# Softcap attention followed by a layer of attention experts: keys transposed by DMA, two pairs of heads at a time, from the eleventh pair on

## The chip, the cores and the metric

The kernel runs on one core of one Trainium2 chip, as one program with one launch. The metric is device microseconds of an execution; lower is better. The time of a kernel is the median of several executions.

## The reference

The first part is attention with a soft cap, for 8 batches of 12 heads with 448 positions and 64 columns a head. Its output is the input x of the second part, a layer of four attention experts with causal attention; a gate picks two of the four for each position.

```python
# part 1: q, k, v are (8, 12, 448, 64) float32, cap = 30
scores = scale * q @ k.T                      # scale = 1 / sqrt(64)
scores = cap * tanh(scores / cap)
attn   = softmax(scores)
x      = (attn @ v).transpose(0, 2, 1, 3).reshape(8, 448, 768)

# part 2: four experts e, 64 columns each
logits = x @ w_gate                           # (8, 448, 4)
topk   = the two largest of the four;  w = softmax over these two
for e in range(4):
    q, k, v = x @ wq[e], x @ wk[e], x @ wv[e]
    a  = softmax(causal(scale * q @ k.T))
    ye = a @ v @ wo[e]                        # (8, 448, 768)
    out += (e in topk) * w[e] * ye
```

The output is (8, 448, 768) in float32.

## The kernel before, in words

**Pairs.** Part 1 goes by pairs of heads: 6 pairs a batch, 48 in all, numbered from 0. A pair goes through these steps. Its q, k and v are loaded by DMA on SyncE's queue (SP), two pairs with one set of DMAs, into four staging buffers (`load`). GpSimd (POOL) casts them to 16 bits: the first 384 positions of the keys (`k16`, L620), q (`q16`, L623), the 64 positions that are left of the keys of both heads as one tile of 128 columns (`ktz`, L635), and v likewise (L639, L644). `tr` then turns q and the keys on TensorE, four transposes of q (L653) and four of the keys (L663: three blocks of `k16` and one of `ktz`), into one PSUM bank, from which VectorE copies 960 columns to a buffer `qk` (L683): 448 columns of q, then 512 of keys. There are six such buffers.

**Scores and exponentials.** `fill` issues the score matmuls from `qk` (`heads` L717, `tails` L727) into two PSUM regions, X of three banks and Y of two. ScalarE reads them with tanh (L768), three instructions a pair: X with 1344 columns, Y with 896, Y again with 896. The exponential of the whole pair follows as one instruction of 3136 columns (`expo`, L780), between two of the next pair's tanh. `pv` multiplies with v on TensorE (L795, L802) and VectorE divides by the row sums (L823, L826); `xt` turns the result on TensorE (L841) and copies it (L850), which gives x with its columns on the partitions.

**Batches.** When the six pairs of a batch are done, part 2 of that batch is spread over the pairs that follow: values and gate logits (`b_v`, L910), the gate on VectorE and POOL (`b_gate`, L974 to L986), a mask that holds the gate weights, cast on POOL (L1028) and turned by a DMA transpose to `mT`; queries and keys of two experts at a time (`b_qk`, L937, the queries then multiplied with the mask, L951); the causal scores of one slot of two experts (`b_score`, L1057) into banks of region X; their exponential on ScalarE (L1066); the product with the values (`b_pv`, L1116, L1131), the sum of two experts on POOL (L1141) that a DMA transpose turns to `oT`; the output product (`b_wo`, L1164), its copies to `ob` (L377) and the stores (L1178). The helper `turned` (L389) issues both kinds of DMA transposes on SP's queue: eight blocks of 128 by 128 in one DMA for a mask, four for an output sum.

At which pair a slot's scores and exponential stand is set by a table: slots 0 and 1 of a batch come at the offsets 5 and 6 after the batch's end, for batch 6 at 6 and 7, which is pair 48 and pair 49:

```python
XOFF = (5, 6)
exps = {HP * (b + 1) + (XOFF if b < LB - 1 else (6, 7))[s]: (b, s) for b in range(LB) for s in range(2)}
```

**The last batch.** Pairs 42 to 47 have only their first 320 query columns in region X and Y; the 128 columns that are left of each go three pairs at a time through two pseudo-pairs, 48 and 49. After them `last` and `last2` do part 2 of the last batch, with a closing chain of copies and stores.

**Order.** No instruction stands where the source text has it. Each step is recorded as an operation with its engine, an assumed duration, what it reads and writes and, for some, a due time relative to one of ScalarE's tanh instructions (`ref`). ScalarE's tanh and exponentials are a fixed chain. From that chain `G.dues` derives due times for the rest, and `G.solve` then makes one list of instructions for each engine: it takes, of the operations that are ready first, the one with the smallest rank, which is the due time with a few constants and with a small shift that is drawn from `SEEDS`, one number for each 4 us. The engines run these lists in order, and semaphores hold an instruction until its inputs are there and its buffer is free. So a change in the constants, the due times or `SEEDS` moves instructions anywhere in the kernel, but each engine still does the same work.

The functions that the change touches, and what calls them:

Of the kernel before, what the change touches and what calls it, by code (L numbers as in the profile page):

```python
# [22 lines left out]
SEEDS = (0, 0, 677, 325, 935, 794, 478, 0, 0, 908, 702, 455, 94, 0, 415, 476, 0, 612, 697, 64, 320, 0, 337, 707, 93, 0, 0, 917, 365, 771, 130, 0, 644, 11, 733, 810, 0, 8, 0, 0, 56, 391, 495, 0, 0, 0, 0, 0, 0, 579, 0, 0, 472, 59, 74, 554, 0, 0, 795, 949, 933, 285, 781, 323, 0, 548, 585, 976, 176, 0, 938, 86, 0, 0, 687, 0, 992, 980)  # L23
TWIRE = 0.2
TOCC = 0.18
# [3 lines left out]
KEEPN = 1  # L29
NFILL = 30  # L30
# [19 lines left out]
class Graph:  # L50
# [79 lines left out]
    def solve(self, when, banks, lent):  # L130
# [44 lines left out]
        while len(order) < n:  # L175
            best = None
            for e, rs in ready.items():
# [8 lines left out]
                def rank(x):  # L186
# [3 lines left out]
                    d = u.due + lag if u.first or left < TAIL else max(u.due + lag, t0 + 1.223)  # L190
                    d -= 0.505 * (u.grp is not None and not u.opens and left >= TAIL)
# [5 lines left out]
                near = t0 + (0.007 if left >= TAIL else SWITCH + 0.02)  # L197
                t, o = min((x for x in c if x[0] <= near), key=rank)
                if e in ("PE", "DVE") and not o.first:
                    for t2, u in c:  # L200
                        if u.first and u.due + lag < t + o.occ + 0.0 and t2 < t + max(SWITCH + 0.01, min(o.occ, 0.25)):
                            t, o = t2, u
                            break
# [66 lines left out]
def kernel(  # L270
# [116 lines left out]
    def turned(n, dst, src, r, w, name, due=None):  # L387

        sp(lambda: nc.sync.dma_start_transpose(  # L389
            dst().rearrange("p (n t) -> p n t", t=128), src()), r, w, due, name,  # L390
           wire=TWIRE * n, occ=0.4 + TOCC * n)

# [11 lines left out]
    vtz = [sb(f"vtz{i}", [128, 2, Dh + 1]) for i in range(NV)]  # L404
    qk = [sb(f"qk{i}", [128, S + 512]) for i in range(NQK)]
# [59 lines left out]
    def load(p, n):  # L465
# [13 lines left out]
        def tail(eng, dst, src, g):  # L479
# [4 lines left out]
        sp(lambda: full(kf[s][:, d], k[b, h, 0:KM], KC), w=w("kf"), name=f"ldk{p}", wire=0.8 * n)  # L484
        sp(lambda: nc_eng.dma_start(qf[s][:, d], q[b, h].rearrange("h (p c) d -> p h (c d)", c=QC)),
           w=w("qf"), name=f"ldq{p}", wire=0.95 * n)
# [8 lines left out]
        sp(lambda: full(vf[s][:, d], v[b, h, 0:KM], KC), w=w("vf"), name=f"ldv{p}", wire=0.8 * n)  # L495
# [119 lines left out]
    def cast(p):  # L615
# [5 lines left out]

        def qc(e):
# [6 lines left out]
        else:  # L629
            gp(0.45, lambda: kc(nc.gpsimd.tensor_copy), *kio, name=f"k16_{p}")  # L630
        if p < 4:
            dve(0.48, lambda: qc(nc.vector.tensor_copy), *qio, name=f"q16_{p}", lat=0.56)
        else:
            gp(0.56, lambda: qc(nc.gpsimd.tensor_copy), *qio, name=f"q16_{p}")
        gp(0.2, lambda: nc.gpsimd.tensor_copy(ktz[z], ktf[s][:, o].rearrange("p g d -> p (g d)")),  # L635
           [("ktf", x, 0), ("ktf", x, 1), ("zk", s)], [("ktz", z)], name=f"kt16_{p}")
# [10 lines left out]
    def tr(p):  # L647
# [29 lines left out]
        g = Group(AUX)  # L677
        pe(0, lambda: tk(g, (0, 1, 2)), kr + [("s", XB[0])] * (p == 1), [("tps", p, "k"), ("qkw", t)], g, occ=0.165, name=f"trk{p}")
# [27 lines left out]

    def heads(p, what):
        dst = X if what == "X" else Y
        ci = {"X": 0, "Y1": 1, "Y2": 2}[what]
        t = qk[of(p, what)[0] % NQK]  # L710
        n = wid(p)
        for c in (ci,) if p < NP else range(KC):
            for g in range(2):
# [4 lines left out]
                    dst[:, g, o], t[r, S + 128 * (c + 1) : S + 128 * (c + 2)], t[r, qs],  # L718
# [3 lines left out]
    def tails(p):  # L722
        for i, m in enumerate(of(p)):
# [3 lines left out]
            nc.tensor.matmul(X[:, 2, o], t[:, S : S + 128], t[:, qs], start=True, stop=True)  # L727

    def fill(p, what):
        def rd(p, what=None):  # L730
            return [y for m in of(p, what) for y in (
                ("qk", m % NQK, "k"), ("qk", m % NQK, "q"), ("qkw", m % NQK))]
# [12 lines left out]
        if what == "X":  # L745
            if p == 0:
                tr_first_tails()
            pe(wid(p), lambda: tails(p), rd(p) + [
                ("qk", m % NQK, "t") for m in of(p)], [("s", bs[2])], name=f"sT_{p}",
# [6 lines left out]
    exps = {HP * (b + 1) + (XOFF if b < LB - 1 else (6, 7))[s]: (b, s) for b in range(LB) for s in range(2)}  # L756
# [145 lines left out]
    def b_v(b, ref):  # L902
        x = b % 2
        for n in range(4):
            g = Group(AUX + XB, 1.8)
            w = WIN[n]
            for j0 in (0, 2, 4):
                def mm(g=g, w=w, j0=j0):
# [8 lines left out]
                   due=(ref, 7.024 + 1.4 * n))  # L917
# [9 lines left out]
    def b_qk(b, ref):  # L927
        x = b % 2
        for r in range(2):
            for which in "kq":  # L930
                g = Group(AUX + XB, 2.4)
                w2 = (wq2 if which == "q" else wk2)[r]
                for j in range(NDC):
                    def mm(g=g, w2=w2, j=j, which=which):
# [10 lines left out]
                        due=(ref, 11.967 + 4.327 * r + 1.8 * (which == "q")))  # L945
# [293 lines left out]
    def last(ref):  # L1239
# [79 lines left out]
        for n in range(3):  # L1319
# [5 lines left out]
            def mm(g=g, n=n):  # L1325
                for e in range(E):
# [11 lines left out]
                   [(b, 3, "z")]), None, WIN1[n], (ref, 8.13))  # L1338
# [45 lines left out]
    def last2(ref):  # L1384
# [63 lines left out]
        for e in range(E):  # L1448
# [3 lines left out]
               gt2[3][:, 1, 0], W1, (ref, 9.393))  # L1452
# [15 lines left out]
    for p in range(NPV):  # L1468
# [13 lines left out]
        for what in order:  # L1482
            if what == "Y2" and p:
# [4 lines left out]
                xt(p - 1, (ACTS["Y1", p], 4.87))  # L1488
# [85 lines left out]
```

## Time and profile before

| | |
|---|---|
| runs | 315.44, 311.67, 313.27 us; median 313.27 |
| profiled execution | span 312.0 us, time 314.04 us |
| busy: TensorE | 280.9 us, 90% |
| busy: VectorE | 217.8 us, 70% |
| busy: ScalarE | 291.8 us, 94% |
| busy: GpSimd | 181.4 us, 58% |
| DMA queue q1 | 65.5% of 16 engines' span |
| HBM | 36.19 MB read, 11.01 MB written |
| granted TensorE clock, mean | 0.983 |

All profile times are from the start of the span, in microseconds, unless marked ns. The profile shows one execution, whose own time is the span and some 2 us around it; it is not the median of the runs. PE is TensorE's matmuls, PEld its weight loads, DVE VectorE, ACT ScalarE, POOL GpSimd, SP SyncE (SPq its queue). A row of an engine's groups reads: line, engine, operation, output and inputs with the shape, the number of instructions, busy time and mean nanoseconds of one, and last the idle time in front of them with what ended it. A row of the waits reads: waiting engine, what it waits to do, what released it, total wait, number, longest. A row of a window reads: the window and its length, then busy time and number of instructions of PE, PEld, DVE, ACT and POOL, the granted clock, the DMA share and the rate in GB/s; where it is asked for one line alone, only the engines that run this line have a column. A row of the timeline reads: start, duration, engine, line, operation, and in brackets the wait that went before.

### The profile page before, as it was taken

To read this page: it belongs to the slowest core of one execution; us is meant where nothing else is said; L and a number is where in the kernel's file an instruction comes from. 1 tells how busy PE (TensorE), PEld (TensorE's weight loads), DVE (VectorE), ACT (ScalarE), POOL (GpSimd) and SP (SyncE) were. 2 spreads that over 40 slices of the span, in tenths; PEclk is the share of its full clock that TensorE was granted. 3 is DMA by queue.
4 is the path that set the end of the run, shared out by engine and by line. 5 is a ranking of instruction groups with operands and counts; after the bars stand their busy time and mean duration, and the time that the engine had idled before them with its cause. 6 is when DMAs were issued, how large, how long until landed. Compare 5 with 4: busy or idle time off the path is not lost.

```text
span 312.0 us, 8950 instructions
## 1 busy us (share of the span) xinstructions
PE 280.9 (90%) x3476; PEld 190.4 (61%) x3476; DVE 217.8 (70%) x645; ACT 291.8 (94%) x246; POOL 181.4 (58%) x498
## 2 busy tenths in 40 slices
PE   7677689979898899989998999999999989999993
PEld 3354356658564766657655776568664866667761
DVE  2345556666764886869766877788776877786883
ACT  4699999998999999999999999999999999999562
POOL 7694436996787452984785576947866414701200
PEclk9979979998999999999999999999999999999999
DMA  6899999869976995789873698855014200531136
GB/s 183 182 227 221 297 272 253 220 168 268 251 189 159 313 272 159 187 179 255 217 164 78 201 310 196 129 162 154 2 41 146 97 2 19 87 120 60 36 148 207
DMA packets 87482, 53.29 MB, mean 171 GB/s; under 512 B 48144, under 2 KB 83728, under 8 KB 87440
## 3 DMA queue, kind: packets, MB, share of 16 engines
q1 hardware_dynamic: 87136, 52.49, 65.5%
q8 instruction: 27, 0.44, 0.6%
q10 hardware_dynamic: 304, 0.23, 0.2%
q14 instruction: 15, 0.12, 0.2%
HBM read 36.19 MB, written 11.01 MB: 151 GB/s over the span
## 4 chain that ended last, share of the span: by engine, by line
ACT 66%; PE 20%; DMA 4%; POOL 3%; issue 3%; DVE 2%; SPq 1%; ACTq 0%; POOLq 0%
ACT yp L768 34%; ACT yp L780 28%; ACT pB L1066 4%; PE A L1164 2%; DMA kf<-in_k_dram 2%; PE Y L717 2%; PE A L937 2%; PE A L910 2%; PE A L802 2%; DMA out_dram<-ob 2%; PE X L1057 1%; PE A L1116 1%; PE A L663 1%; PE A L795 1%; PE X L727 1%
## 5 line engine op out<-in xcount | busy, mean ns | idle before, releaser
L780 ACT ACTIVATE yp<-yp 128x3136 f16<-128x3136 f16 (+4 forms) x51 | 139.0, 2726 | 0.0
L768 ACT ACTIVATE yp<-Y 128x896 f16<-128x896 f32 (+2 forms) x100 | 94.6, 946 | 2.6 <-PE Y L717 2.6
L768 ACT ACTIVATE yp<-X 128x1344 f16<-128x1344 f32 (+2 forms) x50 | 65.1, 1302 | 2.5 <-PE X L727 1.5
L802 PE MATMUL A<-v,yp 128*128 128x65 f16 x1116 | 56.4, 194 | 0.0
L802 PEld LDWEIGHTS <-yp 128*128 128x128 f16 x1116 | 49.0, 98 | 5.7 <-issue 2.9
L795 PE MATMUL A<-vtz,yp 128*128 128x130 f16 x186 | 41.3, 222 | 7.9 <-ACT yp L780 3.7
L826 DVE TENSOR_TENSOR xk<-A,rca 128x256 f16<-128x256 f32 (+1 forms) x96 | 39.7, 415 | 2.9
L717 PE MATMUL Y<-qk 64*128 64x448 f16 (+2 forms) x216 | 36.2, 341 | 5.7 <-ACT yp L768 5.1
L639 POOL CAST v<-vf 128x384 f16<-128x384 f32 x48 | 24.6, 514 | 27.0 <-PE A L802 22.1
L620 POOL CAST k<-kf 128x384 f16<-128x384 f32 x47 | 23.7, 513 | 24.2 <-PE A L663 15.0
L683 DVE COPY qk<-A 128x960 f16<-128x960 f16 x47 | 29.5, 650 | 6.1 <-PE A L653 6.0
L377 DVE COPY ob<-A 128x384 f32<-128x384 f32 (+1 forms) x56 | 30.4, 554 | 4.7 <-PE A L1164 2.9
L823 DVE RECIPROCAL rca<-A 128x4 f32<-128x4 f32 (+1 forms) x96 | 17.1, 178 | 21.0 <-PE A L802 19.4
L795 PEld LDWEIGHTS <-yp 128*128 128x128 f16 x186 | 18.1, 97 | 19.7 <-ACT yp L780 9.3
L623 POOL CAST q<-qf 112x512 f16<-112x512 f32 x44 | 27.2, 619 | 2.3 <-DMA qf<-in_q_dram 2.1
L717 PEld LDWEIGHTS <-qk 64*128 64x128 f16 x324 | 15.0, 93 | 21.7 <-issue 15.5
L1164 PE MATMUL A<-wo,oT 128*128 128x384 f16 x112 | 26.2, 326 | 1.4 <-DVE xT L850 0.5
L1131 DVE SCALAR_TENSOR_TENSOR oB<-A,rcb,mw 128x256 f16<-128x256 f32 x54 | 25.5, 481 | 1.8
L850 DVE COPY xT<-A 128x448 f16<-128x448 f16 (+1 forms) x48 | 18.0, 376 | 9.9 <-PE A L841 9.5
L1141 POOL TENSOR_TENSOR oS<-oB,oB 128x512 f16<-128x512 f16 x14 | 16.1, 1154 | 14.5 <-DVE oB L1131 8.7
L1116 PE MATMUL A<-vB,pB 128*128 128x260 f16 x133 | 22.2, 275 | 1.6 <-DVE oB L1131 1.2
L653 PE MATMUL A<-ident,q 112*128 112x112 f16 x192 | 22.5, 219 | 0.0
(210 smaller groups left out, 569.8 us busy)
## 6 DMA issues: line engine op xcount, KB each, us to landing
qf<-in_q_dram SPq DMA_DIRECT2D x23, 448.0 KB, 6.0
kf<-in_k_dram SPq DMA_DIRECT2D x23, 384.0 KB, 5.2
vf<-in_v_dram SPq DMA_DIRECT2D x23, 384.0 KB, 4.9
out_dram<-ob SPq DMA_DIRECT2D x23, 384.0 KB, 3.8
out_dram<-ob SPq DMA_DIRECT2D x9, 192.0 KB, 2.9
ktf<-in_k_dram SPq DMA_DIRECT2D x46, 32.0 KB, 4.9
vtf<-in_v_dram SPq DMA_DIRECT2D x46, 32.0 KB, 4.3
ob<-in_moe_wv_dram SPq DMA_DIRECT2D x2, 384.0 KB, 4.1
```

The costliest lines, as they stand in the source:

```text
L377: (nc.scalar.copy if o.eng == "ACT" else nc.vector.tensor_copy)(dst(), src())
L623: e(q16[i], qf[s][:, h].rearrange("p h (c d) -> p c h d", c=QC))
L683: lambda: nc.vector.tensor_copy(qk[t], bank16(g)[:, 0 : S + 512]),
L717: nc.tensor.matmul(dst[:, g, o], t[r, S + 128 * (c + 1) : S + 128 * (c + 2)], t[r, qs], start=True, stop=True,)
L768: ACTS[what, p] = act(c_act(n * (b - a)), lambda: nc.scalar.activation(y[:, a:b, 0:n], src[:, 0 : b - a, 0:n], AF.Tanh, scale=isc / capf), ...
L780: act(c_act(n * (b - a), False), lambda a=a, b=b, n=n: nc.scalar.activation(y[:, a:b, 0:n], y[:, a:b, 0:n], AF.Exp, scale=capf), ks, ks, f ...
L795: nc.tensor.matmul(ps[:, n, :, :], y[:, 2, w : w + 128], vtz[u], start=(n == 0), stop=False, skip_group_check=True,)
L802: nc.tensor.matmul(ps[:, n, h, :], y[:, SLOT[c][h], w : w + 128], v16[u][:, h, c, :], start=False, stop=(c == 2), skip_group_check=True,)
L826: dve(c_dve(128 * m), lambda g=g, i=i, rc=rc, m=m: nc.vector.tensor_tensor(xk[p % NXK][:, 2 * i : 2 * i + m, :, :], view(g)[:, 0:m, :, 0:D ...
L1116: nc.tensor.matmul(bank(g)[:, 0 : E * (Dh + 1)], pB[pi][:, o : o + 128], vB[x][:, c, :, :], start=(t == 0), stop=(t == len(cs) - 1),)
L1131: dve(c_dve(E * Dh) + 0.06, lambda g=g, k_=k_, n=n: nc.vector.scalar_tensor_tensor(oB[s][:, n, :, :], view(g)[:, :, 0:Dh], rcb[k_][:, 0, : ...
L1164: nc.tensor.matmul(bank(g)[:, 0 : D // 2], oT[x][n // 2][:, r, n % 2, :], wo2[r][:, c0:c1], start=(r == 0), stop=(r == 1),)
```

## The change

**Keys.** From pair 10 on (`KD = 10`), keys are not turned on TensorE. At every even pair POOL casts the keys of this pair and of the next into one buffer `kz` of two pairs (`kcast`, two casts a pair, of the sizes that they had), and one DMA transpose of 8 blocks on SP's queue turns both pairs into a buffer `kd`. There are two buffers `kz` and three `kd`, and 19 such transposes. For these pairs `tr` has the four transposes of q alone, and the copy from PSUM has 448 columns; the score matmuls read the keys from `kd` and q from `qk`. Pairs 0 to 9 stay as they were.

**Batch 6.** Its first slot is exponentiated at pair 47, before at pair 48.

**Order.** `SEEDS` and the planner's constants are new, among them the assumed time of a DMA transpose on SP and on the DMA engines, and some due times: batch values, queries and keys, `xt`, the output product and two of the last batch. All orders are computed anew from these.

```diff
-SEEDS = (0, 0, 677, 325, ...
-TWIRE = 0.2
-TOCC = 0.18
+SEEDS = (0, 0, 321, 0, ...
+TWIRE = 0.065
+KD = 10
...
-                    d = u.due + lag if u.first or left < TAIL else max(u.due + lag, t0 + 1.223)
-                    d -= 0.505 * (u.grp is not None and not u.opens and left >= TAIL)
+                    d = u.due + lag if u.first or left < TAIL else max(u.due + lag, t0 + 1.213)
+                    d -= 0.269 * (u.grp is not None and not u.opens and left >= TAIL)
...
-                near = t0 + (0.007 if left >= TAIL else SWITCH + 0.02)
+                near = t0 + (0.0 if left >= TAIL else SWITCH + 0.02)
...
-                        if u.first and u.due + lag < t + o.occ + 0.0 and ...
+                        if u.first and u.due + lag < t + o.occ + 0.141 and ...
...
-           wire=TWIRE * n, occ=0.4 + TOCC * n)
+           wire=TWIRE * n, occ=1.25)
...
+    kz = [sb(f"kz{i}", [128, 2, 512]) for i in range(2)]
+    kd = [sb(f"kd{i}", [128, 2, 512]) for i in range(3)]
...
+        def kcast(p):
+            s, o, x, j = p // 2 % NST, p % 2, p % (2 * NST), p // 2
+            dst = kz[j % 2][:, o]
+            gp(0.45, lambda: nc.gpsimd.tensor_copy(
+                dst[:, 128:].rearrange("p (c h d) -> p c h d", h=2, d=Dh),
+                kf[s][:, 2 * o : 2 * o + 2].rearrange("p h (c d) -> p c h d", c=KC)),
+                [("kf", x)], [("kz", j % 2, o, "k")], name=f"k16_{p}")
+            gp(0.2, lambda: nc.gpsimd.tensor_copy(
+                dst[:, 0:128], ktf[s][:, o].rearrange("p g d -> p (g d)")), ...
...
-        else:
+        elif p < KD:
             gp(0.45, lambda: kc(nc.gpsimd.tensor_copy), *kio, name=f"k16_{p}")
+        elif p % 2 == 0:
+            kcast(p)
+            kcast(p + 1)
+            j = p // 2
+            turned(8, lambda: kd[j % 3].rearrange("p o c -> p (o c)"),
+                   lambda: kz[j % 2].rearrange("p o c -> p (o c)"),
+                   [("kz", j % 2, o_, y) for o_ in range(2) for y in "kt"], [("kd", j % 3)],
+                   f"kT{p}")
...
+        if p >= KD:
+            pe(0, lambda: tq(g, 0, 2), ...
+            pe(0, lambda: tq(g, 2, 4), ...
+            dve(c_dve(S, True), lambda: nc.vector.tensor_copy(qk[t][:, 0:S], bank16(g)[:, 0:S]), ...
+            return
...
+    def keysT(p):
+        return qk[p % NQK][:, S:] if p < KD else kd[p // 2 % 3][:, p % 2]
...
-                    dst[:, g, o], t[r, S + 128 * (c + 1) : S + 128 * (c + 2)], t[r, qs],
+                    dst[:, g, o], kT[r, 128 * (c + 1) : 128 * (c + 2)], t[r, qs],
...
-    exps = {HP * (b + 1) + (XOFF if b < LB - 1 else (6, 7))[s]: (b, s) for b in range(LB) for s in range(2)}
+    exps = {HP * (b + 1) + (XOFF if b < LB - 1 else (5, 7))[s]: (b, s) for b in range(LB) for s in range(2)}
...
-                   due=(ref, 7.024 + 1.4 * n))                              # b_v
+                   due=(ref, 5.158 + 1.4 * n))
-                        due=(ref, 11.967 + 4.327 * r + 1.8 * (which == "q")))   # b_qk
+                        due=(ref, 11.882 + 5.017 * r + 1.8 * (which == "q")))
-                xt(p - 1, (ACTS["Y1", p], 4.87))
+                xt(p - 1, (ACTS["Y1", p], 4.366))
-                        b_wo(bb, ACTS["Y1", p], *((12.261, 1.8) if bb < LB - 1 else (10.346, 0.5)))
+                        b_wo(bb, ACTS["Y1", p], *((13.886, 1.8) if bb < LB - 1 else (20.0, 0.5)))
```

37 lines of the change are left out of this document (24 added, 13 removed).

## The prediction

> **What bounds the kernel now.** I read the page's busy times first, then ScalarE's waits, then its timeline, then the windows of the end.
>
> ```profile
> span 312.0 us, 8950 instructions
> ...
> PE 280.9 (90%) x3476; PEld 190.4 (61%) x3476; DVE 217.8 (70%) x645; ACT 291.8 (94%) x246; POOL 181.4 (58%) x498
> ```
> ```profile
> ACT yp L768 <- PE Y L717: 2.6, 2, 1.7
> ...
> ACT yp L768 <- PE X L717: 0.9, 1, 0.9
> ...
> ACT pB L1066 <- PE X L1057: 0.7, 1, 0.7
> ```
> ```profile
> 11.59 0.92 ACT L768 ACTIVATE yp<-Y 128x896 f16<-128x896 f32 x1 [1.69 <-PE Y L717]
> ```
> ```profile
> 58.39 2.87 ACT L780 ACTIVATE yp<-yp 128x3136 f16<-128x3136 f16 x1
> ...
> 63.86 2.89 ACT L780 ACTIVATE yp<-yp 128x3136 f16<-128x3136 f16 x1
> ...
> 75.00 1.29 ACT L768 ACTIVATE yp<-X 128x1344 f16<-128x1344 f32 x1 [0.95 <-PE X L717]
> ```
> ```profile
> 273.02 2.18 ACT L780 ACTIVATE yp<-yp 128x2240 f16<-128x2240 f16 x1
> ...
> 277.26 2.21 ACT L780 ACTIVATE yp<-yp 128x2240 f16<-128x2240 f16 x1
> 280.13 1.02 ACT L1066 ACTIVATE pB<-X 128x1024 f16<-128x1024 f32 x1 [0.66 <-PE X L1057]
> ...
> 289.16 0.88 ACT L780 ACTIVATE yp<-yp 128x768 f16<-128x768 f16 x1
> ```
> ```profile
> 276.00:288.00 12.00, 11.45 (x200) 9.17 (x196) 9.20 (x32) 11.34 (x11) 1.53 (x4) 1.00 0.33 117
> 288.00:300.00 12.00, 12.00 (x139) 8.63 (x137) 9.76 (x41) 7.62 (x19) 2.26 (x2) 1.00 0.10 23
> 300.00:312.00 12.00, 7.17 (x80) 4.17 (x77) 7.00 (x22) 4.93 (x11) 0.00 (x0) 0.98 0.66 231
> ```
> The page is of one execution. Three stages are to be seen. Until 11.59 us ScalarE waits for its first scores, and the change starts at pair 10, so this stage stays. From 11.59 to 290.04 (289.16 + 0.88) ScalarE runs tanh and exponential without pause, 5.47 us a pair (63.86 less 58.39). Its idle time there is 0.95 at 75.00, 0.66 at 280.13, and hardly anything else: about 1.7 us in 278. Then 22 us of end work follow, in which PE is full (12.00 of 12) from 288 to 300 and a chain of copies and stores after 300. So work taken from PE and VectorE in the middle pays only where it ends one of these waits, or empties PE after 276.
>
> **The change part by part.** First, what leaves PE and VectorE: from pair 10 on, 38 pairs no longer pass four key transposes through PE, and their PSUM copy shrinks from 960 to 448 columns.
>
> ```profile
> L663 PE MATMUL A<-ident,k 128*128 128x128 f16 x144 | 16.3, 224 | 4.0 <-POOL k L620 2.1 <-DVE ob L377 0.7 <-DVE oB L1131 0.4
> L663 PE MATMUL A<-ident,ktz 128*128 128x128 f16 x47 | 10.7, 227 | 0.0
> ```
> ```profile
> L683 DVE COPY qk<-A 128x960 f16<-128x960 f16 x47 | 29.5, 650 | 6.1 <-PE A L653 6.0
> L674 DVE COPY qk<-A 128x448 f16<-128x448 f16 x1 | 0.4, 392 | 0.7 <-PE A L653 0.7
> ```
> PE was busy 27.0 us with 191 of these; 152 of them go, by the same mean 21.5 us at most (busy times of neighbours overlap, so less). VectorE saves 38 times 650 less 392 ns, 9.8 us. Both lie beside the unbroken ScalarE stretch, so I count nothing for them in the middle. If that cover were gone, 0.26 us a pair would be VectorE's share of the gain.
>
> Second, what is added: 19 transposes of 8 blocks on SP's queue. The casts on POOL stay as many and as large; only their place in POOL's order changes. The masks' transposes have the same shape and give the price.
>
> ```profile
> L389 SPq DMA_TRANSPOSE mT<-mB x14: 1232/1258/2520, 60.1 to 269.4; - x14
> ...
> DMA to landing us min/median/max: 2.3/2.8/5.7
> ```
> ```profile
> q1 hardware_dynamic: 2656, 0.66, 49.5%
> ```
> ```profile
> q1 hardware_dynamic: 87136, 52.49, 65.5%
> ```
> SP needs 19 times 1.26, 24 us more, spread over 200. The second fence is the DMA view from 266 to 274 us, where two and a half such transposes took 49.5% of 8 us, 3.96 us, so 1.6 us each; 19 are 30 us, a tenth of the span on top of 65.5%. What hides it is lead. There are three key buffers of two pairs each, so a transpose may start once the scores of the fifth pair before it are done and is due four pairs later, 22 us, of which landing takes 2.8 to 5.7. While that lead holds, ScalarE pays nothing. In the new order q's casts, PE's q transposes and the loads stand roughly where they stood.
> [...]
>
> Third, batch 6's first exponential moves from pair 48 to pair 47. The 0.66 wait at 280.13 goes. In its place ScalarE will ask for the scores when the exponential before it ends, at 275.20 (273.02 + 2.18).
>
> ```profile
> 264.32 1.15 POOL L1141 TENSOR_TENSOR oS<-oB,oB 128x512 f16<-128x512 f16 x1
> ...
> 266.88 2.29 POOL L1028 CAST mB<-ms 128x512 f16<-128x512 f32 x4
> ```
> ```profile
> 274.72 1.16 DVE L951 TENSOR_TENSOR qm<-A,mT 128x448 f16<-128x448 f32 x2 [0.79 <-PE A L937]
> ```
> ```profile
> 276.00:282.00 6.00, 1.39 (x18) 1.05 (x18) 1.00 0.63 220
> ```
> The last fence is the score matmuls of L1057 alone. Today the last masked query is ready at 275.88 and the scores take 1.39, so 277.27: unimproved, ScalarE would wait 2.07. The new order puts the 1.15 us addition behind the masks instead of into the gate, issues ten of the last twelve query matmuls before the second tanh's scores of pair 47 and gives batch 6's values an earlier due time (5.158 after 7.024). With 1.15 saved the wait is 0.92; with the PE order too it may be none. I take 0.3, bounds 0 and 2.07. Everything behind that instruction on ScalarE, two tanh of pairs 47 and 48 first, and so PE's next fills, would move with it.
> Those 1.39 us of PE also leave the window 276 to 282, just before PE is full. Of them 0.66 is the wait already counted; of the other 0.73 I take 0.4, since about as many output matmuls of batch 5 now come later (their offset goes from 12.261 to 13.886). Bounds 0 and 0.73. Further in, the gate's small exponential now stands before the last tanh on ScalarE and may wait some tenths; left in the range.
>
> Fourth, the new order elsewhere. The 0.95 at 75.00 hangs on the order of that stretch; half of it, 0.5, is taken as gain, bounds 0 and 0.95. Against it stands the clock.
>
> ```profile
> 31.64:35.06 3.42, 2.03 (x35) 1.29 (x34) 2.05 (x7) 3.42 (x3) 0.96 (x2) 1.00 1.14 323
> ...
> 38.47:41.88 3.41, 1.97 (x31) 1.44 (x32) 1.15 (x5) 3.41 (x5) 1.51 (x4) 1.00 0.94 279
> 41.88:45.30 3.42, 3.26 (x21) 1.95 (x21) 2.36 (x7) 3.42 (x4) 1.13 (x3) 0.50 1.06 302
> ...
> 65.78:69.19 3.41, 1.81 (x28) 1.25 (x25) 2.83 (x10) 3.41 (x4) 3.09 (x11) 1.00 0.66 182
> 69.19:72.60 3.41, 3.41 (x40) 2.87 (x38) 1.72 (x5) 3.41 (x3) 1.11 (x5) 0.50 0.91 240
> ...
> 137.46:140.87 3.41, 2.53 (x23) 1.44 (x23) 2.29 (x6) 3.41 (x5) 2.38 (x8) 1.00 0.77 173
> ```
> ```profile
> 137.46:140.87 3.41, 0.48 (x4) 0.34 (x4) 1.00 0.77 173
> ```
> These are steps of 3.41 us. One with PE busy 1.97 or 1.81 is followed by one at half clock, one with 2.03 is not. The half-clock step at 69.19 stands right before the 0.95 wait; the one at 41.88 cost ScalarE nothing. So a further half-clock step costs 0 to 0.95. The step at 137.46 would fall from 2.53 to 2.05 without its key transposes (second fence), almost to the edge. I count 0.3, a third of one such wait.
> [...]
>
> The sum: -0.66 + 0.3 - 0.4 - 0.5 + 0.3 = -0.96. The profiled execution has span 312.0 and time 314.04, 2.0 around the span; it becomes 311.0 and 313.1. That execution lies 0.8 above the median 313.27, so the median goes to **312.3**.
>
> **The rivals.** One, slower: keys late through SP's queue. In the new order key transposes stand directly behind mask and output transposes, and loads behind them.
>
> ```profile
> SPq L389 <- POOL oS L1141: 41.4, 5, 14.0
> SPq L389 <- POOL mB L1028: 24.1, 7, 4.7
> ```
> SP already stands up to 14.0 us at such a wait. The lead less landing is 16 to 19 us; where 14.0 and one more wait of 4.7 come together, 18.7, the keys miss their pair by up to 2.5 us and ScalarE stands that long. Two such places give 5.0, and with -0.96 a time of 317.3. For it speaks that a held transpose holds the loads too; against it, that 14.0 arose at the end with nothing queued behind. It decides from a hold of 16 us.
>
> Two, slower: the clock. Four more half-clock steps at 0.95 instead of 0.3 in the sum give +3.5 and 315.8; two give 313.9. For: the step at 137.46. Against: the lightest steps after 72 us hold few key transposes, and two of three drops cost nothing.
>
> Three, faster: all waits after 11.59 end and PE's relief counts in full: 0.66 + 0.95 + 0.73 and the further 0.2 of small gaps, 2.5, giving 310.7; with 0.6 more in the closing chain, 310.1.
>
> Four, the change does not do what it says: batch 6's first scores are not ready a pair sooner. ScalarE waits 2.07 instead of 0.66, +1.4 and no gain in the tail, 314.7 with nothing else gained.
>
> **How the numbers follow.** Chances: forecast 0.48, keys late 0.16, clock 0.10, all waits gone 0.18, not ready 0.08. ScalarE's unbroken stretch holds the gain to about 1%; only a loss can be large. About 1%, 3.1 us, is what a measurement of this kernel tells from no change (its three runs go from 311.67 to 315.44). Faster by more than that: all of the third rival's better half and a little of the forecast, 0.19. Slower: keys late and half of the clock case, 0.22. Within: 0.59. The range goes from 309.6 (the third rival less half a microsecond of spread) to 316.8 (most of the first).
>
> **What would show it.** Right: ScalarE still spaced 5.47 a pair; no wait on a key transpose among ScalarE's and PE's waits; batch 6's first exponential right behind the exponential of pair 46, its wait under 1 us; the PSUM copies near 392 ns; 47 transposes of some 1.26 us on SP with landing near 2.8. Wrong: ScalarE waiting for scores whose PE instruction waits for DMA; more half-clock steps than three before the end; PE's full stretch after 288 longer than 12 us. If ScalarE's last exponential ends later than 290, the forecast of a gain is wrong whatever the end does.

## The result, and the profile after

The changed kernel is slower: 326.69 us (median of 4 runs, 325.7 to 327.89) against 312.47 us in the same runs (311.39 to 315.44), a ratio of 1.0441 [1.0357, 1.0525]. The forecast was 312.3. Medians here and below are of all executions, while ratios leave out the few in the chip's slower state, so that a ratio need not be the quotient of two medians.

From the page: its span, the busy times, the granted clock by slices and the row of the DMA queue:

```profile
span 324.6 us, 8665 instructions
...
PE 278.3 (86%) x3324; PEld 181.8 (56%) x3324; DVE 207.8 (64%) x643; ACT 293.7 (90%) x248; POOL 181.7 (56%) x498
...
PEclk9999999989799799999959999999999999999999
...
q1 hardware_dynamic: 107200, 57.47, 72.7%
```

PE and DVE do less, and the busy share of every engine is lower than before: the kernel waits more. The queue's packets took 72.7% of 324.6, 236.0 us, where they took 65.5% of 312.0, 204.4 us.

ScalarE's waits, with the last exponentials of its main stretch:

```profile
ACT yp L803 <- PE Y L751: 14.2, 13, 3.4
...
ACT yp L803 <- PE X L751: 2.2, 3, 1.7
```
```profile
298.65 1.05 ACT L1101 ACTIVATE pB<-X0X1s 128x1024 f16<-128x1024 f32 x1
...
300.35 2.58 ACT L815 ACTIVATE yp<-yp 128x1920 f16<-128x1920 f16 x2
```

ScalarE now ends its stretch at 302.93, before at 290.04: 12.9 us later. The rest of the span is 21.7 us, before 22.0. So the whole loss lies ahead of the last exponential, and nearly all of it is waits for scores: 14.2 and 2.2 us, where before they came to 2.6 and 0.9. Without those of the first 12 us they are 14 waits with 14.5 us, where the kernel before has 0.95 and 0.66.

Where they stand, in the windows of 60 us (PE, PEld, DVE, ACT, POOL busy, clock, DMA share, GB/s), first of the kernel before, then of the changed one:

```profile
60.00:120.00 60.00, 53.90 (x684) 37.78 (x682) 41.77 (x120) 59.05 (x45) 43.02 (x111) 0.97 0.87 229
120.00:180.00 60.00, 56.89 (x712) 38.40 (x710) 46.47 (x129) 59.79 (x45) 38.67 (x98) 1.00 0.72 180
180.00:240.00 60.00, 57.30 (x705) 39.15 (x702) 45.76 (x135) 59.99 (x47) 42.97 (x108) 1.00 0.57 142
```
```profile
60.00:120.00 60.00, 50.02 (x585) 33.25 (x583) 35.84 (x109) 53.97 (x41) 36.84 (x96) 0.91 0.99 230
120.00:180.00 60.00, 48.70 (x546) 30.69 (x543) 35.87 (x110) 51.66 (x39) 37.33 (x94) 0.94 0.91 218
180.00:240.00 60.00, 55.07 (x698) 37.65 (x697) 45.30 (x138) 59.87 (x46) 37.66 (x93) 1.00 0.62 155
```

ScalarE loses 6.0 us of 60 and then 8.3, and nothing from 180 on. These are the two windows in which the DMA share is highest (0.99 and 0.91) and the clock falls. A high share alone does not make ScalarE wait, as `e15_free_keys` shows further down.

Two waits, followed back. First through the casts, in the changed kernel's timelines of POOL, PE and ScalarE:

```profile
119.37 0.51 POOL L627 CAST kz<-kf 128x384 f16<-128x384 f32 x1 [3.71 <-DMA kd<-kz]
...
123.12 0.52 POOL L1111 TENSOR_SCALAR_AFFINE_SELECT pB<-pB 128x384 f16<-128x384 f16 x1
```
```profile
122.11 0.27 PE L677 MATMUL A<-ident,q 112*128 112x112 f16 x2 [0.81 <-POOL q L637]
...
123.70 0.28 PE L1151 MATMUL A<-vB,pB 128*128 128x260 f16 x1 [1.02 <-POOL pB L1111]
```
```profile
122.72 0.92 ACT L803 ACTIVATE yp<-Y 128x896 f16<-128x896 f32 x1 [0.54 <-PE Y L751]
...
129.17 0.92 ACT L803 ACTIVATE yp<-Y 128x896 f16<-128x896 f32 x1 [0.85 <-PE Y L751]
```

A key cast on POOL waits 3.71 us for an earlier transpose that has not yet read its cast buffer. Behind it in POOL's order stand q's casts and the causal selection of `pB`; behind these on PE stand scores that need neither. Second, through the output transposes, where POOL's addition `oS`, SP and PE follow each other:

```profile
125.88 1.15 POOL L1176 TENSOR_TENSOR oS<-oB,oB 128x512 f16<-128x512 f16 x1 [0.57 <-DVE oB L1166]
```
```profile
130.68 2.26 SPq L389 DMA_TRANSPOSE kd<-kz  x1
133.03 1.21 SPq L389 DMA_TRANSPOSE oT<-oS  x1
```
```profile
137.83 0.50 PE L1199 MATMUL A<-wo,oT 128*128 128x384 f16 x2 [2.89 <-DMA oT<-oS]
```

The sum is done at 127.03; SP is behind and issues its transpose at 133.03, 6.0 us late and right behind a key transpose. In the kernel before, the same step goes from one to the other in 0.03 us (118.47 + 1.15 = 119.62, then 119.65):

```profile
118.47 1.15 POOL L1141 TENSOR_TENSOR oS<-oB,oB 128x512 f16<-128x512 f16 x1 [0.94 <-DVE oB L1131]
```
```profile
119.65 1.23 SPq L389 DMA_TRANSPOSE oT<-oS  x1
```

The clock falls in the same stretch: five half-clock steps stand between 60 and 180 us (from 64.70, 85.20, 105.66, 163.69 and 167.10), where the kernel before has one (from 69.19). In the step ahead of three of them PE had stood 1.7 to 2.3 us for an operand from POOL or a DMA; ahead of the first there is no wait that long, and the last follows another half-clock step. No run isolates what these steps add to the loss. The dearest wait of ScalarE, 3.40 us at 91.00, lies behind this pair:

```profile
81.79:85.20 3.41, 1.49 (x12) 0.84 (x14) 1.28 (x5) 3.37 (x2) 1.24 (x4) 1.00 0.97 223
85.20:88.61 3.41, 3.41 (x18) 2.00 (x15) 1.64 (x6) 2.10 (x2) 3.19 (x6) 0.50 1.11 310
```

### The profile page after: what moved, and what is told of

Read it like the earlier page. It is cut to its first block, busy times and chain, and to the rows that moved or that the text cites. A ratio compares the mean times of both kernels' runs of the same rounds, so it can differ in the third digit from the quotient of the medians.

```text
span 324.6 us, 8665 instructions
## 1 busy us (share of the span) xinstructions
PE 278.3 (86%) x3324; PEld 181.8 (56%) x3324; DVE 207.8 (64%) x643; ACT 293.7 (90%) x248; POOL 181.7 (56%) x498
## 3 DMA queue, kind: packets, MB, share of 16 engines
q1 hardware_dynamic: 107200, 57.47, 72.7%
## 4 chain that ended last, share of the span: by engine, by line
PE 19%; ACT 16%; POOL 6%; DMA 6%; DVE 6%; issue 3%; POOLq 0%; DVEq 0%
ACT yp L803 8%; ACT yp L815 6%; DMA kd<-kz 3%; PE A L1199 3%; PE A L837 2%; PE A L972 2%; DMA mT<-mB 2%; DVE ob L377 2%; PE Y L751 2%; ACT pB L1101 2%; POOL mB L1063 1%; PE A L830 1%; PE A L1151 1%; PE A L945 1%; PE A L876 1%
## 5 line engine op out<-in xcount | busy, mean ns | idle before, releaser
L803 ACT ACTIVATE yp<-Y 128x896 f16<-128x896 f32 (+2 forms) x100 | 93.1, 931 | 14.3 <-PE Y L751 14.2
L837 PE MATMUL A<-v,yp 128*128 128x65 f16 x1116 | 57.1, 196 | 0.0
L837 PEld LDWEIGHTS <-yp 128*128 128x128 f16 x1116 | 49.9, 99 | 7.4 <-issue 4.8
L637 POOL CAST q<-qf 112x512 f16<-112x512 f32 x44 | 26.1, 613 | 15.3 <-PE A L677 6.9
L627 POOL CAST kz<-kf 128x384 f16<-128x384 f32 x38 | 18.7, 508 | 24.8 <-DMA kd<-kz 16.4
L751 PE MATMUL Y<-qk,kd 64*128 64x448 f16 (+2 forms) x176 | 28.8, 337 | 2.0 <-ACT yp L803 1.8
L830 PEld LDWEIGHTS <-yp 128*128 128x128 f16 x186 | 18.3, 98 | 21.0 <-ACT yp L815 9.8
L677 PE MATMUL A<-ident,q 112*128 112x112 f16 x192 | 18.5, 217 | 8.8 <-POOL q L637 4.9
L945 PE MATMUL A<-wvg,xT 128*128 128x260 f16 x168 | 24.3, 293 | 0.3 <-DVE xT L885 0.3
L945 PEld LDWEIGHTS <-xT 128*128 128x128 f16 x168 | 16.6, 104 | 7.3 <-issue 3.5
```

The lines of the kernel that those rows point to most:

```text
L637: e(q16[i], qf[s][:, h].rearrange("p h (c d) -> p c h d", c=QC))
L751: nc.tensor.matmul(dst[:, g, o], kT[r, 128 * (c + 1) : 128 * (c + 2)], t[r, qs], start=True, stop=True,)
L803: ACTS[what, p] = act(c_act(n * (b - a)), lambda: nc.scalar.activation(y[:, a:b, 0:n], src[:, 0 : b - a, 0:n], AF.Tanh, scale=isc / capf), ...
L830: nc.tensor.matmul(ps[:, n, :, :], y[:, 2, w : w + 128], vtz[u], start=(n == 0), stop=False, skip_group_check=True,)
L837: nc.tensor.matmul(ps[:, n, h, :], y[:, SLOT[c][h], w : w + 128], v16[u][:, h, c, :], start=False, stop=(c == 2), skip_group_check=True,)
L945: nc.tensor.matmul(bank(g)[:, 0 : E * Dh + E], xT[x][:, j, w : w + 128], wvg[:, j, :], start=(j == 0), stop=(j == NDC - 1),)
```

## Experiments

The theory after this reading: the transposes cost through SP's queue and the DMA engines, which have too little room from 60 to 180 us. The rivals: the new order by itself, PE's clock, and the buffers of the keys alone. All runs but the replanned ones keep the order of their kernel on every engine, so that only the edit differs. Edits are shown shortened, partly in words. Ratios are to the kernel before, with 95% intervals.

### The transposes taken out, and put into the kernel before

`e1_undo`, the keys back on TensorE in the changed kernel's order:

```diff
-            turned(8, kd[j % 3] <- kz[j % 2])            # kT
+            kT is an empty operation
-   PE: tq(0, 2); tq(2, 4)            DVE: copy of 448 columns, keys from kd
+   PE: tq(0, 2); tq(2, 4), td(4 blocks of kz)   DVE: copy of 960 columns, keys from qk
```


> The changed kernel with the same order on every engine, but the 19 key transposes on the DMA queue are left out and the keys of pairs 10 to 47 are turned on TensorE again, out of the same cast buffers and right behind the transposes of q, with the PSUM copy of 960 columns. If the DMA transposes cost the time (by the hold of POOL's key casts, by SP's queue or by the DMA engines): near the time of before, 312 to 315 us. If the new order by itself costs it: 323 to 328. If PE's lighter load and so its clock cost it: also near before, but with at most 2 half-clock steps between 60 and 180 us where the changed kernel has 5.

Measured: 317.2 us, 1.0153 [1.0087, 1.0218]. So 9.5 of the 13 to 14 us come and go with the route of the keys, and some 4 are left.

`e4_before_extra`, 19 transposes of nothing in the kernel before:

```diff
         full(vf[s][:, d], v[b, h, 0:KM], KC)
+        if p >= 10:
+            nc.sync.dma_start_transpose(zd[p // 2 % 3], zs)   # 8 blocks of a constant
```


> The kernel before, same order, with 19 DMA transposes of 8 blocks of a constant buffer added on SP, each behind a load of v, waiting for nothing but earlier DMAs and awaited by nothing. If the transposes' time on SP and on the DMA engines alone makes loads late: 316 to 326 us. If only their place among the waits costs: within 1.5 us of before, 311 to 314.

Measured: 329.0 us, 1.0488 [1.0422, 1.0553]. Nobody waits for these transposes and no cast buffer is held, yet they cost 15 to 16 us. PE's waits for `oT` tell how, in the row of the waits, together with what the transposes themselves took to land:

```profile
PE A L1171 <- DMA oT<-oS: 10.6, 5, 4.7
```
```profile
DMA to landing us min/median/max: 3.9/5.7/7.4
```

This is the strongest run of the study: key data, the keys' buffers, TensorE's lighter load and the new order are all out of it.

### Buffers and clock

`e2_kz4` gives the casts four buffers, `e3_kz4_kd6` also six buffers of turned keys:

```diff
-    kz = [... for i in range(2)]          kd = [... for i in range(3)]
+    kz = [... for i in range(4)]          kd = [... for i in range(6)]     # the second in e3 only
```


> The changed kernel with the same order, but four cast buffers for key pairs instead of two, so that POOL's key casts no longer wait until an earlier DMA transpose has read its buffer (16.4 us in 7 waits, and 4.5 us more at 102.9 us). If this hold is the cause: ScalarE's waits at 122.72, 129.17, 162.90 and 171.63 us (0.54, 0.85, 1.66, 1.94) go, some 5 us, 321 to 322 us. If transposes and loads are late through SP's queue or busy DMA engines instead: 325 to 328.

> The changed kernel with the same order, four cast buffers and six buffers of turned keys instead of three, so that SP no longer holds a key transpose until PE has read old keys. If holds through buffers, on POOL and on SP, are the whole cause: 313 to 316 us. If it is busy DMA engines or the number of instructions on SP: 321 to 328.

Measured: 322.96 us, 1.0328 [1.0274, 1.0382], and 324.11 us, 1.0364 [1.0319, 1.041]. The hold of POOL's casts is worth some 3.7 us. More buffers of turned keys give nothing on top. Holds through buffers are a part, not the cause.

`e7_dummy_pe` gives PE four dummy transposes a pair in place of the ones that left:

```diff
+            for c in range(4):
+                nc.tensor.transpose(bank16(g)[:, S + 128 * c : S + 128 * (c + 1)], ident, ident)
             tq(g, 0, 2)
```


> The changed kernel, same order, with four dummy transposes of the identity ahead of each pair's q transposes from pair 10 on, in place of the key transposes that left TensorE; their output is never read. If the lighter load of TensorE and so its clock is a large part of the loss: at most 2 half-clock steps between 60 and 180 us where there were 5, and 318 to 323 us. If the clock only follows the late transfers: 325 to 330.

Measured: 327.61 us, 1.0441 [1.039, 1.0491]. It has three half-clock steps from 60 to 180 us instead of five (and two right after), so the count missed the line that was drawn, but the time did not move. In the step ahead of one of them PE stands behind a late operand, and busy time ahead of the wait can't fill all of it:

```profile
80.80:84.21 3.41, 0.70 (x6) 0.43 (x7) 0.67 (x3) 3.41 (x2) 2.92 (x8) 1.00 1.05 284
84.21:87.63 3.42, 3.38 (x16) 1.63 (x16) 1.80 (x6) 1.91 (x3) 2.88 (x6) 0.50 1.03 301
```

This run alone does not dismiss the clock. Filler is work too: TensorE's real key transposes, with their longer PSUM copies, cost 5.5 us in the same order (`e1_undo` against `e15_free_keys`), and an unmoved time may hide a gain of up to that size. Plainer evidence is `e15_free_keys`: there TensorE turns no keys either, nothing is added to it, and the granted clock is 1.00 in each window of 60 us from 60 to 240. So the lighter TensorE does not bring the half-clock steps by itself.

### SP's queue or the DMA engines

In the kernel before, `e5_before_issue` puts two DMAs of 2 KB where `e4_before_extra` had a transpose, `e6_before_engines` one more load of q:

```diff
         if p >= 10:
+            for y in range(2): nc.sync.dma_start(zt[p // 2 % 3 * 2 + y], zs[0:16, :])   # e5
+            nc.sync.dma_start(zq[p // 2 % 3][:, d], q[b, h] as loaded)                  # e6
```


> The kernel before, same order; where the earlier run added a DMA transpose of 8 blocks (329.0 us), two DMAs of 2 KB stand, awaited by nothing. They take SP about as long to issue (2 x 0.6 us for 1.26) and almost no time of the DMA engines. If SP's issue time makes the others late: 322 to 329 us. If the time of the DMA engines does: 312 to 316.

> The kernel before, same order; in the same 19 places one more load of q, 448 KB, into a buffer that nothing reads. By an estimate from the queue's time (204 us for 47 MB of copies and 168 blocks at 0.24 us) it takes the DMA engines 1.6 us, near the 1.9 us of 8 transposed blocks, and SP 0.6 us to issue instead of 1.26. If the DMA engines' time is the cause: 322 to 329 us. If SP's issue time is: 313 to 318. If a transpose as such holds up the copies around it, whatever its size: 313 to 318 too.

Measured: 322.96 us, 1.0303 [1.0261, 1.0345], and 332.94 us, 1.0628 [1.0568, 1.0688]. Each was to cost much only if its own resource was the cause, and both did: SP's issues alone cost 10 us, more of the engines' time (with 19 issues of half the length) 20. In the first the engines are no busier than in the kernel before, 0.88 and 0.72:

```profile
60.00:120.00 60.00, 49.85 (x652) 34.37 (x651) 39.89 (x116) 56.56 (x44) 40.48 (x107) 1.00 0.88 219
120.00:180.00 60.00, 51.47 (x585) 33.57 (x585) 38.72 (x110) 52.60 (x40) 35.31 (x88) 0.94 0.72 171
```

The load was also dearer than my estimate: the queue's row of that run, 76.5% of 330.4 us, is 48.4 us more than before, 2.5 us for each of 19 loads instead of 1.6, if all of it is put down to them. Nor is SP busy without a pause in the first run: its issues, summed over its timeline, take some 54 of 60 us and then 44 (47 and 38 in the kernel before), and ScalarE loses more in the second window (7.4 us) than in the first (3.4). What costs is that DMAs which others wait for come later in the line: the issues of `oT` by 23.0 us in all, where the kernel before has 3.3 (table below).

The same question in the changed kernel, by relief: `e13_sp_relief` leaves out v's tail loads, `e14_engine_relief` halves the loads of q and v (both from pair 10 on, with stale data in their place):

```diff
-        tail_("vtf", vtf, v, "zv")
+        tail_("vtf", vtf, v, "zv")  if p < KD                                  # e13
-        load q, v of heads h        (two pairs, four heads)
+        load q, v of heads h[0:2]   if p >= KD                                 # e14
```


> The changed kernel, same order, key transposes kept; left out are the two tail loads of v of each two pairs from pair 10 on (32 KB each, v's tail is stale). This frees SP of 38 issues, some 24 us, as much as the 19 transposes take, and frees little of the DMA engines' time (1.2 MB, in small packets). If SP's queue is what the transposes take: 316 to 320 us. If the DMA engines are: 323 to 327.

> The changed kernel, same order, key transposes kept, every DMA still issued; from pair 10 on the loads of q and v bring only two of four heads (the rest is stale). By the queue's own rate (0.288 MB a us) this frees 1.5 us of the DMA engines for each two pairs, 28 us in all, near the 37 us of the transposes, and nothing of SP. If the DMA engines are what the transposes take: 316 to 320 us. If SP's queue is: 323 to 327. If both must be free: each of the two runs gains some 3 to 5 us.

Measured: 314.64 us, 1.005 [1.0017, 1.0082], and 313.68 us, 0.9998 [0.9958, 1.0038]. Either relief alone takes back 12 to 13 us; I had expected one of them to, or a few us from each. The first leaves the engines as full as in the changed kernel:

```profile
60.00:120.00 60.00, 53.28 (x657) 35.83 (x655) 39.89 (x124) 60.00 (x46) 43.81 (x112) 1.00 1.06 258
120.00:180.00 60.00, 53.78 (x644) 34.85 (x643) 42.87 (x123) 58.20 (x45) 38.43 (x99) 0.97 0.91 213
```

and the second leaves SP all its issues. Both also drop or shorten loads that the casts wait for, so they relieve what came late as well as what made it late. My reading: SP and the engines are two stations of one pipeline, and what ran out is its common slack.

One measure goes with the loss through these runs. It is the time from the end of an output sum on POOL to the issue of its transpose `oT` on SP, added up over the 14 sums from each run's timelines:

| run | delay of the 14 sums, us | ratio of the times |
|---|---|---|
| kernel before | 3.3 | 1 |
| changed kernel | 19.6 | 1.0441 |
| `e4_before_extra` | 33.0 | 1.0488 |
| `e5_before_issue` | 23.0 | 1.0303 |
| `e6_before_engines` | 24.8 | 1.0628 |
| `e13_sp_relief` | 11.4 | 1.005 |
| `e14_engine_relief` | 10.0 | 0.9998 |
| `e15_free_keys` | 6.4 | 0.9956 |

In these orders a late line on SP goes with a slow kernel, whichever of the two was loaded. What passes the slack from one to the other isn't shown. In the traces of the kernel before and of the changed one, with 242 and 261 DMAs on SP, none starts before the one eight issues earlier has landed (28 and 20 start before the one seven earlier has), so longer landings could hold the issues. But SP seldom stands for that alone: between 60 and 180 us, idle time of SP that ended within 0.25 us of such a landing comes to 0.0 us in `e4_before_extra` and 1.8 in `e5_before_issue`, and to 5.9 in `e15_free_keys`, which loses nothing. So this limit is not what costs in the first two; in `e6_before_engines`, with 9.8 us, it may be a part.

`e8_split32` uses the DMA only for pairs 32 to 47, in the changed kernel's order; the others as in `e1_undo`:

```diff
-            kT by DMA for every even p >= 10
+            kT by DMA for even p >= 32; pairs 10 to 31 on TensorE
```


> The changed kernel, same order, where pairs 10 to 31 turn their keys on TensorE as in the first run of this study (317.2 us for all pairs) and only pairs 32 to 47 by DMA, 8 transposes in place of 19, all after the stretch from 60 to 180 us in which the DMA engines are full. If the full DMA engines are the cause: 315 to 318.5 us, no more than without any. If each transpose costs wherever it stands: 8/19 of the 9.5 us, about 321.

Measured: 318.25 us, 1.0141 [1.0088, 1.0194], beside 317.2 without any. Eight of the 19 transposes are as good as free late in the kernel, where the DMA share is 0.55 (180 to 240 us of this run) and SP has pauses too: its issues take at most 31 of these 60 us.

### What there was to gain

`e15_free_keys` (changed kernel) and `e16_before_free_keys` (kernel before) turn the keys of pairs 10 to 47 nowhere; the scores read the cast keys as they lie, so the output is no longer attention:

```diff
-    keys from kd, or from qk by way of TensorE and PSUM
+    keys = the cast buffers (six of two pairs; in the kernel before eight of one pair)
```


> The changed kernel, same order, where keys from pair 10 on are turned by nothing: neither DMA nor TensorE, the score matmuls read the cast keys as they lie, out of six buffers. So it shows the order without the price of the transposes. If the 4 us left over in the first run were TensorE's key transposes in an order that has no room for them: 311 to 314 us. If the order itself is slower: 315 to 318.

> The kernel before, same order, where keys from pair 10 on are turned by nothing and read as they lie, out of eight cast buffers; the PSUM copies have 448 columns. This is all that the relief of TensorE and VectorE could bring if the DMA side were free. By the prediction's reading (only the waits of ScalarE and the end count): 310.5 to 313. If a lighter TensorE falls into half-clock steps: 313 to 318. If TensorE was a hidden bound: under 309.

Measured: 311.67 us, 0.9956 [0.9928, 0.9983], and 311.4 us, 0.9968 [0.9936, 0.9999]. ScalarE's last main exponential with free keys, and with keys on TensorE in the same order (`e1_undo`):

```profile
285.03 2.58 ACT L816 ACTIVATE yp<-yp 128x1920 f16<-128x1920 f16 x2
```
```profile
289.73 2.58 ACT L823 ACTIVATE yp<-yp 128x1920 f16<-128x1920 f16 x2
```

The stretch from 60 to 120 us of `e15_free_keys` belongs beside that of the changed kernel: the same order and the same DMA share, and ScalarE loses nothing.

```profile
60.00:120.00 60.00, 53.25 (x656) 35.87 (x655) 40.16 (x125) 60.00 (x46) 43.41 (x111) 1.00 0.99 246
```

The share of 0.99 is thus reached by the new order without one key transpose, and a share near 1 can't be read as a loss; `e5_before_issue` lost its 10 us at an unchanged one.

Keys that cost nothing at all are worth 0.3 to 0.4%. Put together, turning the keys of pairs 10 to 47 costs:

(medians of different sets of runs, the kernel before taken at 312.9)

| | order of before | new order |
|---|---|---|
| not at all | 311.4 | 311.7 |
| on TensorE | 312.9, +1.5 | 317.2, +5.5 |
| by DMA | not run | 326.7, +15.0 |
| on TensorE, and 19 transposes by DMA | 329.0, +17.6 | not run |

With free keys the new order is no worse than the old. What `e1_undo` left over, 4 us, is the price of TensorE's transposes and VectorE's longer copies in an order that has no room for them; the two cast buffers, which `e1_undo` has and `e15_free_keys` does not, hold POOL for only 0.7 us there.

### Orders computed anew

`e9_after_order_KD48`, `e10_old_order_KD10`, `e11_old_order_KD32` and `e12_before_slot` let the planner work again:

```diff
 e9:  changed kernel   -KD = 10        +KD = 48
 e10: kernel before    +keys by DMA, KD = 10      e11: the same with KD = 32
 e12: kernel before    -(6, 7))[s]     +(5, 7))[s]
```


> The changed kernel with KD = 48: no key transposes by DMA, keys of all pairs on TensorE as before; new due times, constants and batch 6's earlier slot stay, and the orders are computed anew from them, so that the order fits the work. If the 4 us that were left in the first run (317.2 us) come from an order made for a lighter TensorE: 312 to 315 us. If the new constants and due times are worse by themselves: 316 to 320.

> The other half: keys by DMA from pair 10 on, with SEEDS, constants, due times, load costs, assumed transpose times and batch 6's slots of before; orders computed anew. If full DMA engines and SP's queue cost the time whatever the order: 322 to 332 us. If the new order is needed to lose no more: over 332. If the new constants are the fault: 312 to 317.

> As the last, with KD = 32: keys by DMA only for pairs 32 to 47, in the stretch where the DMA engines were 57% busy before. If transposes in that stretch cost nothing: 311 to 315 us, no gain either, since TensorE isn't what ScalarE waits for. If each costs wherever it stands: 318 to 322. A gain below 311 would say that a lighter TensorE is worth something late in the kernel.

> The kernel before with batch 6's first slot at pair 47 in place of 48, its own constants, orders computed anew. If the earlier slot ends the 0.66 us wait at 280.13 us and empties TensorE a little before the end, as the prediction counted: 311.5 to 313, ScalarE's wait before that exponential under 1 us. If the scores aren't ready: its wait is some 2 us and the time 313.5 to 315.

Measured: 325.84 us, 1.0389 [1.0337, 1.0441]; 326.41, 1.0396 [1.0332, 1.0461]; 315.5, 1.0069 [1.003, 1.0109]; 317.34, 1.0138 [1.0083, 1.0192]. The first settles nothing on the DMA: without a single key transpose it loses 12 us, so an order that is merely computed anew can lose as much as the transposes do. In the second, one wait of ScalarE late in the kernel, for scores that stood behind other work of PE, makes up half of the loss (timeline of `e10_old_order_KD10`):

```profile
280.16 0.97 ACT L804 ACTIVATE yp<-X 128x960 f16<-128x960 f32 x1 [6.56 <-PE A L838]
```

So whole-kernel times of replanned orders can't part the change in halves. A window can tell something, though. In the second run the 19 transposes pass through the same stretch, and ScalarE keeps 57.99 and then 59.78 of 60 us, the latter at a DMA share of 1.03:

```profile
120.00:180.00 60.00, 54.11 (x669) 36.59 (x667) 44.07 (x127) 59.78 (x45) 41.09 (x104) 1.00 1.03 241
```

Its output sums are delayed by 19.1 us in all, as much as in the changed kernel, so an order can carry such delays through this stretch. Its planner assumed 0.2 us of the DMA engines for a block, 1.6 us for eight; the changed kernel's `TWIRE` assumes 0.065, which is 0.52 us for eight, where the traces show 1.6 (kernel before) to 1.9 (`e4_before_extra`, 36.9 us more than before for 19). So the 15 us are the price in an order that was made for transposes a third as dear. No run changes that constant alone, and whether an order made with the right price would lose less in all stays open.

The third run, with late transposes only, lands between its two expectations: it loses some 2 us. The last is told below.

No run points to a version that beats the kernel before and turns all its keys: in these two orders the ceiling lies 0.4% below it.

## Why the prediction was wrong, step by step

**What bounds the kernel: right.** ScalarE's stretch and the closing 22 us are what the time is made of, and relief of PE and VectorE is worth next to nothing in the middle (1.5 us in all by `e16_before_free_keys`). The prediction's sum came to 312.3; the kernel with free keys takes 311.67. What was forecast is the time of a change whose transposes cost nothing. That the two lie so close is in part luck, for the terms did not come out one by one: with free keys the wait at 75.00 is gone whole (0.95, counted as 0.5), the slot's scores bring no wait (0.3 counted against the gain), and the gain of 0.4 in the closing part is not there.

**"What hides it is lead ... ScalarE pays nothing": the step that failed.** It was priced at 0 and measured 15.0 in its own order. The sizes were near: 30 us of engine time were counted, and the queue's row shows 31.6 more (30.8 against `e15_free_keys`, which has the same order). For SP's issues 24 us were counted and 29.6 taken, the median at 1.28 but the longest at 3.2; the landing of 2.8 became 3.7:

```profile
L389 SPq DMA_TRANSPOSE kd<-kz x19: 1238/1280/3248, 46.1 to 260.4; - x19
...
DMA to landing us min/median/max: 3.1/3.7/6.7
```

Three things went wrong. First, room was judged by a mean, the share over the span (65.5% and a tenth on top). The stretch from 60 to 120 us stood at 0.87 already, and the loads did not stand "roughly where they stood": the new order by itself brings this stretch to 0.99 (`e15_free_keys`). Since that run loses nothing, the share is not the cost itself, but the DMAs that `e4_before_extra` and `e5_before_issue` add made those behind them late (the issues of `oT` by 33.0 and 23.0 us in all, without them 3.3). Second, the lead was worked out for the keys, and the keys kept it: none of PE's listed waits is for `kd`. What came late were other transfers on the same queue, `oT` and loads, and, through the cast buffers, the casts on POOL; these had no 22 us of lead. Third, the two cast buffers were not looked at. The transposes' reader is the DMA, so a late transpose holds POOL (16.4 us in 7 waits), worth 3.7 us by `e2_kz4`.

**Rival one had the queue right and the victim wrong.** It needed a hold of 16 us before keys missed their pair, and was worth 5.0. The two delays that were followed back are of 3.7 and 6.0 us, on a cast and on `oT`, and ScalarE's loss is 14 waits for scores of which the longest is 3.40 us.

**Rival two, the clock.** Five half-clock steps came where one stood. Three of them follow holds of PE, and `e15_free_keys`, with no key transposes on TensorE, has none between 60 and 240 us. So the lighter load was not the cause; what the steps add once the holds are there isn't isolated. The edge that the prediction saw in PE's busy time of a step, between 1.97 and 2.03 us of 3.41, is not in this trace: a half-clock step follows 1.49 (81.79 to 85.20) and 1.76 (61.29 to 64.70), but none follows 1.76 (132.97 to 136.38) or 1.96 (136.38 to 139.79). What sets off a half-clock step is not shown.

**TensorE or the DMA.** The price of 8 blocks was read from the masks' row and was nearly right: 19 times 8 blocks added 31.6 us of engine time, 1.7 us for eight where 1.6 were counted, and landed in 3.7 where 2.8 were read. By these runs TensorE, at 1.5 to 5.5 us for all keys of pairs 10 to 47, is cheaper than the DMA at 15.0. The cost came from a shared queue, which the price of 8 blocks does not show.

**Batch 6's slot: the wait right, and only in this order; the gain in the end not shown.** The exponential of the slot follows its neighbour with no wait. The closing part, after ScalarE's last exponential, is 21.7 us here, but 21.9 in `e15_free_keys` and 22.1 in `e1_undo`, which have the same slot, against 22.0 before; 0.4 were counted. The slot's lines:

```profile
286.57 2.25 ACT L815 ACTIVATE yp<-yp 128x2240 f16<-128x2240 f16 x1
288.57 1.16 ACT L1101 ACTIVATE pB<-X 128x1024 f16<-128x1024 f32 x1
```

Rival four, the scores not ready, is what the same step does in a replanned order of before (`e12_before_slot`), at 4.38 us and not 2.07:

```profile
278.38 1.02 ACT L1066 ACTIVATE pB<-X 128x1024 f16<-128x1024 f32 x1 [4.38 <-PE X L1057]
```

**The wait at 75.00** is gone, where half was expected (in `e15_free_keys` ScalarE is busy 60.00 of 60 us from 60 to 120); it was worth 0.95 beside 14.5 us of new ones. The signs that were named did their work: ScalarE's last exponential later than 290 was said to refute a gain, and scores that wait behind DMAs were named as a sign of being wrong.

## What to carry to other kernels

Look at an added transfer in the stretch where it runs, and not at the mean of the span: how much of the time the queue's engine is already issuing there, and how late the DMAs behind it may come. The DMA share alone didn't decide here: 0.99 without a loss in `e15_free_keys`, 0.72 with a loss of 7.4 us of ScalarE's time in `e5_before_issue`. Ask of an added DMA not only when its own result is due but what stands behind it on the queue and which engine's buffer it reads, and which of these has the least lead. And when an order is planned, freeze it for experiments: change buffers, add dummy work or leave work out under the same order, since an order computed anew lost up to 4% here with no key transposes by DMA in it.

## What the runs showed that I had not expected

Thirty-eight DMAs of 2 KB that nobody waits for cost 10 us of 313, with the DMA engines no busier than before (0.88 and 0.72 in the two windows from 60 us on, after 0.87 and 0.72) and SP itself not busy throughout (some 54 and 44 of 60 us). Relief of SP's issues alone (38 of them) and relief of the engines alone each took back 12 to 13 us of the same loss of 15: the two weren't parts of a sum. An extra 448 KB load added 2.5 us to the engines' time, where the queue's mean rate had given 1.6. And the same DMA share of 0.99 went with a loss of 6.0 us of ScalarE's time in one run and with none in another.
